# Loads in order of need, attention inside the first second-GEMM, and neighbouring chunks' GEMMs alternated, in a linear-attention plus two-GEMM kernel

## The chip, the cores and the metric

The kernel runs on one core of one Trainium2 chip. The metric is the time of one execution in device microseconds (us), as the median over several runs. In the profile the engines are PE (matrix multiply), PEld (its weight loads), DVE (vector engine), ACT (scalar engine), POOL (GpSimd) and SP (the engine that only issues transfers here). An engine's name with a trailing q (SPq, ACTq) is its transfer queue.

## The reference

Attention with exponential decay over 4 batches, 8 heads, 768 positions and head size 64 gives x, 3072 tokens by 512. Two GEMMs with an activation between them follow.

```python
# attention, per head, equivalent to:  out_i = sum_{j<=i} lam^(i-j) (q_i . k_j) v_j
x = attn_out.transpose(0, 2, 1, 3).reshape(3072, 512)
h = x @ w_in                                  # 512 x 2048
s = np.sin(alpha * h)
g = h + s * s / (alpha + 1e-09)
return (g @ w_out).astype(np.float32)         # 2048 x 512
```

## The kernel before

Tokens are worked in six chunks (c = 0 to 5) of 512. A chunk takes four attention steps of 128 tokens (s = 0 to 23), then 16 groups of GEMM1 (one for each 128 of the 2048 columns), then 16 groups of GEMM2 (4 for each 128 tokens). Every group is four matmuls of 128x512. The program only records operations with what they read and write and an assumed duration. A list scheduler then orders the queue of every engine by assumed readiness, except that PE keeps the program's order; semaphores are added at the end.

One attention step does this on the engines:

```python
def prep(s):                       # (cut to engine and operation)
    POOL: q2 = q32 * Lq            # scalings by powers of lam
    POOL: k2 = k32 * Lk
    ACT:  v2 = v32                 # cast to bf16
def att_T(s):  PE: 8 transposes of q2, k2;  DVE: qkT = copy from PSUM
def att_S(s):  PE: 8 score matmuls;         DVE: S_m = scores * mask
def att_O(s):  PE: output matmuls;          ACT: xT = copy from PSUM
               PE: state matmuls;           ACT: Zs = copy from PSUM (two of them)
```

The GEMM groups (cut):

```python
def grp_A(c, m):                   # GEMM1, one of 16 groups
    i = next_bank()                # ring of 5 PSUM banks
    PE:   m_ps[i] = 4 matmuls of w1, xT
    ACT:  t = sin(alpha * m_ps[i])
    POOL: u = t * t
    DVE:  gT[c % 2][m] = u * r + m_ps[i]
def grp_B(c, s4, m4, bank):        # GEMM2, one of 16 groups
    PE:   m_ps[bank] += 4 matmuls of gT, w2
    if m4 == 3:
        ACT: osb = copy of m_ps[bank]
        SP:  store osb
```

And the order (cut):

```python
load(0); consts(); load(1..3); alpha_ops()
for s in range(4):  prep, att_T, att_S, att_O of step s;  w1_block(s)
load(4); load(5)
for j in range(4): w2_block(j)     # two staging buffers, so block 2 waits for the cast of block 0
for s in range(6, 9): load(s)
for m in range(16): grp_A(0, m)
for m4 in range(4):
    for s4 in range(4): grp_B(0, s4, m4, banks[s4])
for s in range(4, 8): attention of step s          # nothing else for PE here
for c in range(1, 6):
    for m in range(16): grp_A(c, m)                # attention of chunk c+1 in between
    for s4 in range(4):
        bank = next_bank()
        for m4 in range(4): grp_B(c, s4, m4, bank) # alone on PE
```

## Time and profile before

The kernel took 272.02 us (median of three runs, 270.7 to 272.72). The profiled execution had a span of 270.4 us. I divide it by the first matmul of each stage in the timeline of PE.

| stage | from, us | length, us |
|---|---|---|
| before the first GEMM | 0 | 28.5 |
| GEMM1 of chunk 0 | 28.5 | 18.9 |
| GEMM2 of chunk 0, then attention of chunk 1 | 47.4 | 46.8 |
| GEMM1 of chunk 1 (attention of chunk 2 inside) | 94.2 | 23.4 |
| all the rest of PE's work | 117.6 | 149.7 |
| tail (last copy and store) | 267.3 | 3.1 |

These are lines of the profile's page of the kernel before. The first are busy time in us, share of the span and number of instructions of each engine. The digits are the busy share in tenths in 40 slices of the span, 6.8 us each. PEclk is the granted clock of PE in tenths, and GB/s is what the transfers moved. Of a group of instructions (engine, operation, destination, sources, shapes), the figures are the busy time in us and the mean ns of one, then the idle time ahead of them with what ended most of it.

```profile
span 270.4 us, 4030 instructions
PE 222.9 (82%) x1584; PEld 108.9 (40%) x1584; DVE 123.9 (46%) x159; ACT 120.7 (45%) x214; POOL 148.9 (55%) x151
...
PE   0346998822954699899999899999999999999895
...
POOL 1830299990043469990299930899206782069700
PEclk9995599995795579999999999999999999999999
DMA  8999999999999965655230012100121001210022
GB/s 164 220 209 393 240 292 269 205 238 335 209 219 283 229 153 119 156 119 155 78 80 0 2 39 78 41 1 2 40 78 41 0 2 39 78 41 0 0 78 78
...
L458 PE MATMUL m_ps<-w,gT 128*128 128x512 bf16 x384 | 87.1, 386 | 14.8 <-DVE w L343 12.8
```

Three things are to be seen. First (slices counted from 1), PE is partly idle in slices 1 to 4, and slices 9 to 14 hold a second hole. Second, the GEMM2 matmuls (L458) had 12.8 us of idle time that ended with a DVE weight cast. Third, the transfers are busy without a break for the first 95 us, and slices 2 and 3, which hold q, k and v loads, move 220 and 209 GB/s, where slice 4, with w1 blocks, moves 393. The q, k and v loads come in pieces of 256 bytes, the weights in pieces of 2 KB. The Trainium skill ("DMA: Bandwidth & Descriptors", Specifications) states that a transfer needs pieces of at least 512 bytes for the line rate, which these two rates agree with.

This is the chain of waits, which is followed back from the last instruction, for 56.9 to 66.3 us of the kernel before. Columns: start in us, length in us, what it was.

```profile
56.90 8.05 DMA w2s<-in_moe_w_out_dram
...
64.97 1.24 DVE w L343
...
66.25 9.17 PE m_ps L458 x32
```

GEMM2 of chunk 0 stops for its third weight block. After it, from 75.4 to 94.2, chunk 1's attention runs as a chain of short dependent steps with little for PE to do, and the granted clock was 0.54 from 80 to 90 us. The timeline of PE shows that idle time is in brackets:

```profile
76.66 0.40 PE L382 MATMUL A_ps<-qkT 64*128 64x128 bf16 x8 [0.79 <-DVE qkT L373]
78.38 0.40 PE L401 MATMUL A_ps<-qkT,Zs 128*128 128x128 bf16 x4 [1.32 <-DVE S_m L386]
```

In the long rest, GEMM1 is limited by POOL, which has 16 squares of 1.04 us in every chunk and, while the attention of a later chunk is prepared, up to 8 scalings of 1.04 us. The timeline of POOL in the kernel before shows them back to back:

```profile
102.93 1.04 POOL L350 TENSOR_TENSOR q_4<-q_2,Lq 128x512 bf16<-128x512 f32 x1
103.93 1.04 POOL L447 TENSOR_TENSOR u_0<-t_0 128x512 bf16<-128x512 bf16 x1
```

### The profile page before, as it was taken

The page shows a single profiled execution, that of the slowest core. Times are in us where ns is not written, and L with a number is a line of the kernel's source. Part 1 is how long each engine was busy: PE and PEld are TensorE (multiplying, and loading weights), DVE is VectorE, ACT ScalarE, POOL GpSimd, SP SyncE. Part 2 cuts the span into 40 slices and gives each one's busy share as a digit, 9 for nine tenths or more (in the row PEclk, how much of TensorE's full clock was granted, in tenths as well). Part 3 has the DMA queues.
Part 4 walks back from the last instruction along what each step waited for, and adds up shares of the span by engine and source line. Part 5 has one row for each costly group of instructions (what it writes and reads, how often), then busy time and mean ns, then how long its engine had stood idle before and what let it go on. Part 6 is the DMA issues. An engine that isn't in the chain of part 4 may idle for free.

```text
span 270.4 us, 4030 instructions
## 1 busy us (share of the span) xinstructions
PE 222.9 (82%) x1584; PEld 108.9 (40%) x1584; DVE 123.9 (46%) x159; ACT 120.7 (45%) x214; POOL 148.9 (55%) x151
## 2 busy tenths in 40 slices
PE   0346998822954699899999899999999999999895
PEld 0235432310433544444454444545445554443342
DVE  1246378601134358760187810787305893037600
ACT  2433477100132458731387711868216762167211
POOL 1830299990043469990299930899206782069700
PEclk9995599995795579999999999999999999999999
DMA  8999999999999965655230012100121001210022
GB/s 164 220 209 393 240 292 269 205 238 335 209 219 283 229 153 119 156 119 155 78 80 0 2 39 78 41 1 2 40 78 41 0 2 39 78 41 0 0 78 78
DMA packets 84786, 33.82 MB, mean 125 GB/s; under 512 B 77600, under 2 KB 77600, under 8 KB 84768
## 3 DMA queue, kind: packets, MB, share of 16 engines
q1 hardware_dynamic: 84768, 33.57, 51.5%
q8 instruction: 12, 0.20, 0.3%
q14 instruction: 6, 0.05, 0.1%
HBM read 27.28 MB, written 6.29 MB: 124 GB/s over the span
## 4 chain that ended last, share of the span: by engine, by line
PE 49%; POOL 18%; DVE 11%; DMA 7%; ACT 5%; SPq 5%; issue 4%; POOLq 1%; ACTq 0%
PE m_ps L458 25%; PE m_ps L441 15%; POOL u_2 L447 5%; SPq L290 4%; POOL u_1 L447 4%; DVE gT L449 4%; POOL u_0 L447 3%; POOL u_3 L447 3%; DVE S_m L386 3%; DMA w2s<-in_moe_w_out_dram 3%; PE A_ps L382 3%; DVE qkT L373 2%; DMA v_3<-in_v_dram 2%; DMA v_2<-in_v_dram 2%; PE A_ps L405 1%
## 5 line engine op out<-in xcount | busy, mean ns | idle before, releaser
L458 PE MATMUL m_ps<-w,gT 128*128 128x512 bf16 x384 | 87.1, 386 | 14.8 <-DVE w L343 12.8
L441 PE MATMUL m_ps<-xT,w 128*128 128x512 bf16 x384 | 94.4, 392 | 0.8 <-ACT xT L414 0.5
L447 POOL TENSOR_TENSOR u_0<-t_0 128x512 bf16<-128x512 bf16 x24 | 26.0, 1082 | 70.4 <-ACT t_0 L445 69.4
L458 PEld LDWEIGHTS m_ps<-w,gT 128*128 128x128 bf16 x384 | 37.1, 99 | 63.1 <-DVE w L343 14.2
L441 PEld LDWEIGHTS m_ps<-xT,w 128*128 128x128 bf16 x384 | 35.5, 100 | 46.5 <-DVE gT L449 6.9
L386 DVE TENSOR_TENSOR S_m<-A_ps,mask 128x1024 bf16<-128x1024 f32 x24 | 29.4, 1224 | 53.0 <-PE A_ps L382 52.9
L466 ACT COPY osb<-m_ps 128x512 f32<-128x512 f32 x24 | 14.1, 586 | 79.2 <-PE m_ps L458 77.4
L449 DVE SCALAR_TENSOR_TENSOR gT<-u_0,r_sb,m_ps 128x512 bf16<-128x512 bf16 x24 | 17.9, 744 | 24.3 <-POOL u_0 L447 24.2
L447 POOL TENSOR_TENSOR u_1<-t_1 128x512 bf16<-128x512 bf16 x24 | 26.0, 1082 | 1.3 <-ACT t_1 L445 1.3
L447 POOL TENSOR_TENSOR u_2<-t_2 128x512 bf16<-128x512 bf16 x24 | 25.0, 1041 | 1.1 <-ACT t_2 L445 0.6
L447 POOL TENSOR_TENSOR u_3<-t_3 128x512 bf16<-128x512 bf16 x24 | 25.0, 1041 | 0.0
L445 ACT ACTIVATE t_2<-m_ps,alpha_sb 128x512 bf16<-128x512 f32 x24 | 16.5, 687 | 15.0 <-PE m_ps L441 15.0
L449 DVE SCALAR_TENSOR_TENSOR gT<-u_2,r_sb,m_ps 128x512 bf16<-128x512 bf16 x24 | 17.9, 747 | 6.3 <-POOL u_2 L447 6.3
L449 DVE SCALAR_TENSOR_TENSOR gT<-u_1,r_sb,m_ps 128x512 bf16<-128x512 bf16 x24 | 17.9, 746 | 4.9 <-POOL u_1 L447 4.9
L373 DVE COPY qkT<-A_ps 128x1024 bf16<-128x1024 bf16 x20 | 13.7, 686 | 13.9 <-PE A_ps L370 13.9
L445 ACT ACTIVATE t_0<-m_ps,alpha_sb 128x512 bf16<-128x512 f32 x24 | 16.5, 687 | 6.0 <-PE m_ps L441 5.8
L449 DVE SCALAR_TENSOR_TENSOR gT<-u_3,r_sb,m_ps 128x512 bf16<-128x512 bf16 x24 | 17.8, 742 | 2.3 <-POOL u_3 L447 2.3
L445 ACT ACTIVATE t_1<-m_ps,alpha_sb 128x512 bf16<-128x512 f32 x24 | 16.5, 687 | 4.8 <-PE m_ps L441 4.7
L445 ACT ACTIVATE t_3<-m_ps,alpha_sb 128x512 bf16<-128x512 f32 x24 | 16.5, 687 | 4.8 <-PE m_ps L441 4.5
L382 PE MATMUL A_ps<-qkT 64*128 64x128 bf16 x192 | 11.0, 242 | 7.4 <-DVE qkT L373 6.6
L414 ACT CAST xT<-A_ps 128x512 bf16<-128x512 f32 x20 | 11.6, 579 | 11.4 <-PE A_ps L405 11.4
L428 ACT CAST Zs<-Z_ps 64x256 bf16<-64x256 f32 x40 | 14.7, 367 | 0.5
(164 smaller groups left out, 175.5 us busy)
## 6 DMA issues: line engine op xcount, KB each, us to landing
out_dram<-osb SPq DMA_DIRECT2D x24, 256.0 KB, 2.0
w1s<-in_moe_w_in_dram SPq DMA_DIRECT2D x4, 1024.0 KB, 8.5
w2s<-in_moe_w_out_dram SPq DMA_DIRECT2D x4, 1024.0 KB, 8.3
q_0<-in_q_dram SPq DMA_DIRECT2D x4, 256.0 KB, 4.6
k_0<-in_k_dram SPq DMA_DIRECT2D x4, 256.0 KB, 4.3
v_0<-in_v_dram SPq DMA_DIRECT2D x4, 256.0 KB, 5.4
q_1<-in_q_dram SPq DMA_DIRECT2D x4, 256.0 KB, 4.6
k_1<-in_k_dram SPq DMA_DIRECT2D x4, 256.0 KB, 4.9
```

The source lines that it names most:

```text
L290: rec("SP", lambda e, a=a, d=dst[r]: e.dma_start(d[:, :, :], a), 0, writes=[f"{nme}32.{r}"], slot=f"{nme}{r}", nbytes=128 * 2048)
L373: rec("DVE", lambda e: e.tensor_copy(qkT[j][:, :, :], dst), 0.7, reads=[key], writes=[f"qkT.{j}"])
L382: last = e.matmul(A_ps[:, 4 * h + jp, :], qkT[j][rows, 4 + jp, :], qkT[j][rows, jp, :])
L386: rec("DVE", lambda e: e.tensor_tensor(S_m[j][:, :, :], A_ps[:, :, :], mask_b, ALU.mult), 1.25, reads=["S0", "S1", "mask"], writes=[f"S_m. ...
L414: rec("ACT", lambda e: e.copy(xT[x][:, :, col:col + 128], dst), 0.62, reads=[key], writes=[f"x.{x}.{s % 4}"])
L428: rec("ACT", lambda e, rows=rows, cols=cols: e.copy(Zs[j][rows, :, cols], Z_ps[rows, :, :]), 0.4, reads=["Z"], writes=[f"Zs.{j}"])
L441: last = e.matmul(m_ps[i][:, :], w1[:, kc, 128 * m:128 * (m + 1)], xT[x][:, kc, :], start=(kc == 0), stop=(kc == NKC - 1))
L445: rec("ACT", lambda e: e.activation(t16[tt][:, :], m_ps[i][:, :], ACTF.Sin, scale=alpha_sb[:, m:m + 1]), 0.7, reads=[f"m.{i}", "alpha"], w ...
L447: rec("POOL", lambda e: e.tensor_tensor(u16[tt][:, :], t16[tt][:, :], t16[tt][:, :], ALU.mult), 1.05, reads=[f"t.{tt}"], writes=[f"u.{tt}"])
L449: rec("DVE", lambda e: e.scalar_tensor_tensor(out=gT[g][:, m, :], in0=u16[tt][:, :], scalar=r_sb[:, m:m + 1], in1=m_ps[i][:, :], op0=ALU.m ...
L458: last = e.matmul(m_ps[bank][:, :], gT[g][:, m, 128 * s4:128 * (s4 + 1)], w2[:, m, :], start=(m == 0), stop=(m == NM - 1))
L466: rec("ACT", lambda e: e.copy(osb[o][:, :], m_ps[bank][:, :]), 0.6, reads=[f"m.{bank}"], writes=[f"o.{o}"])
```

## The change

The intent is to give PE work where it waits. Loads are put in the order in which they are needed. Chunk 1's attention is placed between the groups of chunk 0's GEMM2. From then on GEMM1 of the next chunk alternates with GEMM2 of this one, so that POOL's work for GEMM1 is spread over twice the matmuls. Smaller parts: four q scalings and eight squares go from POOL to DVE, one staging ring of six serves both weights, alpha arrives as 16 rows and is transposed on PE, the stores are issued by ACT instead of SP, and the output buffers go from three to four.

The core of the diff (cut; the bookkeeping of the soft ordering between loads and the constants' changes are left out; comments after # are mine):

```diff
-            for nme, src, dst in (("q", q, q32), ("k", k, k32), ("v", v, v32)):
+            for nme, src, dst in (("k", k, k32), ("q", q, q32), ("v", v, v32)):
...
-        w1s = ring("w1s", 4, [128, NKC, 512], F32)
-        w2s = ring("w2s", 2, [128, 4, DM], F32)
+        ws = ring("ws", 6, [128, 4, 512], F32)
...
+            dve = c in (0, NCH - 1) and m % 4 == 3
+            rec("DVE" if dve else "POOL",
+                lambda e: e.tensor_tensor(u16[tt][:, :], t16[tt][:, :], t16[tt][:, :], ALU.mult),
+                0.35 if dve else 1.05, reads=[f"t.{tt}"], writes=[f"u.{tt}"])
...
-                rec("SP", lambda e: e.dma_start(out[row0:row0 + 128, :], osb[o][:, :]), 0,
+                rec("ACT", lambda e: e.dma_start(out[row0:row0 + 128, :], osb[o][:, :]), 0,
...
+        for s in range(4):
             load(s)
         alpha_ops()
+        for j in range(4):
+            w1_block(j)
+        for j in range(2):
+            load(4 + j)
+            w2_block(j)
+        loaded = [8]
...
+        def slot_att(base, i, per):      # attention step base + i // per, in parts
+            s = base + i // per
+            if s >= NSTEP:
+                return
+            if i % per == per // 4:
+                att_S(s)
+            elif i % per == per // 4 * 3:
+                att_O(s)
+                if s + 1 < NSTEP:
+                    att_T(s + 1)
+                prep_next(s + 2)         # also issues the next load
...
+            if s < 2:                    # within the steps of chunk 0
+                load(6 + s)
+                w2_block(2 + s)
...
         for m4 in range(4):
             for s4 in range(4):
                 grp_B(0, s4, m4, banks[s4])
+                slot_att(4, 4 * m4 + s4, 4)
+        for m in range(NM):
+            grp_A(1, m)
+            slot_att(8, m, 4)
         for c in range(1, NCH):
+            for i in range(NM):
+                if c + 1 < NCH:
+                    grp_A(c + 1, i)
+                    slot_att(4 * (c + 2), 2 * i, 8)
+                if i % 4 == 0:
+                    bank = next_bank()
+                grp_B(c, i // 4, i % 4, bank)
+                if c + 1 < NCH:
+                    slot_att(4 * (c + 2), 2 * i + 1, 8)
```

## The prediction

> **What bounds the kernel now.** Overview: PE 222.9 of 270.4 us (82%). The chain of waits shows three regimes.
> 1. Start, 0 to 28.5 us: no GEMM. Loads of steps 0-3 (256-byte pieces) move about 215 GB/s (overview, slices 2-3); weight loads reach 393. The Trainium skill ("DMA: Bandwidth & Descriptors", Specifications) asks for pieces of at least 512 B; the trace agrees. Landed inputs wait in order: Lk (7.6 us) behind v_0's cast and lam; qkT of step 2 behind alpha (18.2); xT behind v_3's cast.
> 2. 47 to 94 us: the third w2 block lands only at 65, behind later q/k/v loads: PE idles 10.2 us, returns at half clock (0.51 in 60-70), and chunk 1's attention runs as a bare latency chain from 75.5 to 94.
> 3. GEMM1 with attention and q/k scaling: POOL squares and scales at 1.04 us each, 16+8 are 25 us; three such phases took 26.4, 24.6 and 23.9 us, the fourth, free of scalings, 19.9 at PE's pace. GEMM2 takes 13.9 (217 ns a matmul), POOL mostly idle.
>
> **What changes.** Loads in order of need (alpha and lam off that queue; alpha as 16 rows instead of 2,048 four-byte pieces); four q scalings and 8 squares to DVE; stores issued by ACT; chunk 1's attention inside GEMM2 of chunk 0; GEMM1 of c+1 alternated with GEMM2 of c. Arithmetic is nearly unchanged. PE's warm floor: 768 x 217 ns + 24 x 1.5 us (attention step: (19.9-13.9)/4) = 203 us.
>
> **Estimate, from those durations.**
> - Same load rates: four steps land by 16-17 us, scaling constants come before v_0's cast: first GEMM at 23 (was 28.5).
> - GEMM1 of chunk 0: 12 squares and 3 scalings on POOL, weight casts and gT on DVE: ends near 41.
> - w2 interleaved with steps 4-7, the last lands near 53. GEMM2 with four attention steps, 19.9: ends near 62. Bare attention (18.5 us) and the 10 us wait disappear.
> - GEMM1 of chunk 1: POOL's order puts the scalings of steps 8-11 before its first square; step 11 lands near 68, so PE fills five banks and stalls 3.5 us; then 25 POOL operations: ends near 92 (was 120.8).
> - Three alternating chunks: POOL needs 25 us, PE 33.8: 101.
> - A new wait: the second GEMM gets the same bank each time, so its next group waits for the output copy, which ACT runs behind xT, two Zs and the v cast: estimate 0.5 us per attention step, 6.
> - GEMM1 of 5 with GEMM2 of 4: 28; last GEMM2 14; tail 3.
> Sum 244 us of span, less a little if the copy fits behind a GEMM1 group; time was 1.6 above span. I say 243.
>
> Nearly all is on the critical path, since PE becomes the limit: about 29 us before 121 us, the rest from POOL's slow chunks.
>
> **Predicted:** 243 us, 233 to 252 eight times in ten. Faster by over 2%: 0.97; within 2%: 0.02; slower: 0.01.
>
> **What would show it.** First GEMM at 21-25 us; no later PE gap over 4 us; chunk 1's attention between GEMM2 matmuls; PE above 90% busy from 95 us; alternating chunks at 34-36 us; GEMM2 waits for the ACT copy once per attention step; PE busy 205-215 us, clock 0.5 only before 35 us.
>
> **What would make it wrong.** Store issues on ACT holding up sines; DVE's added two-input work blocking POOL (its square took 2.0 us beside a weight cast, else 1.04), slowing GEMM1 of chunks 0 and 1; steps 8-11 landing after 68, as stores share the engines. Better: no bank wait and no stall before step 11 (about 235).

## The result, and the profile after

The changed kernel took 247.4 us (median of 4 runs, 245.79 to 248.81), beside 272.37 us for the kernel before. The ratio is 0.9092, with a 95% interval of 0.9023 to 0.916. A ratio is the mean time of one kernel's fast runs over the mean time of the other's in the same rounds, so it is not quite the ratio of the medians quoted. The profiled span was 245.2 us. All runs gave correct results. Executions over 1.5% slower than the fastest of the same kernel are left out of the means.

These are the lines of the page after that answer to those shown of before:

```profile
span 245.2 us, 3912 instructions
PE 218.0 (89%) x1560; PEld 107.9 (44%) x1585; DVE 132.2 (54%) x170; ACT 120.9 (49%) x215; POOL 141.9 (58%) x141
...
PE   0576969589989789999999999999999999999994
...
POOL 3220588973739799998668686554454445554100
PEclk9999988959999979999999999999999999999999
DMA  7999999999999799999311011011101100111122
GB/s 147 218 254 389 284 262 255 262 288 244 219 281 242 176 224 220 208 245 209 100 45 43 0 45 44 0 45 43 45 0 43 45 19 23 43 45 43 43 86 86
...
L478 PE MATMUL m_ps<-w,gT 128*128 128x512 bf16 x367 | 93.6, 385 | 1.8 <-ACT osb L486 0.5
```

The second hole of PE is gone: GEMM2's matmuls waited 1.8 us in all. (The attention's score matmuls that now stand between them, L400, waited 6.7 us in the whole kernel; the longest of these waits is taken up below.) From slice 16 on PE is full, and POOL's digits are 6 to 9 up to slice 25 and then 4 or 5 as long as GEMM1 runs, where they swung between 0 and 9 before. The transfers are nearly full until about 116 us (19 slices of 6.1 us), and POOL, the old limit, has spare time. The line of PE has 24 instructions fewer than the 1584 of before because matmul records are missing; the arithmetic is nearly the same.

The view of windows gives the busy time of each engine (and its number of instructions) in each stretch, then the granted clock, the DMA share and GB/s. Read PE, and PEclk. The kernel after, with the stages as its boundaries:

```profile
core 0: us, PE busy (x) PEld busy (x) DVE busy (x) ACT busy (x) POOL busy (x), PEclk, DMA share, GB/s
0.00:24.10 24.10, 11.58 (x141) 8.69 (x143) 12.54 (x19) 10.52 (x23) 5.49 (x13) 1.00 1.08 250
24.10:44.20 20.10, 17.91 (x63) 6.92 (x64) 16.09 (x19) 11.20 (x18) 15.54 (x13) 0.92 0.99 270
44.20:71.80 27.60, 23.16 (x202) 12.17 (x203) 15.96 (x18) 9.20 (x19) 18.22 (x16) 0.88 1.19 256
71.80:96.50 24.70, 21.48 (x196) 11.46 (x200) 16.67 (x22) 18.25 (x35) 21.06 (x22) 0.93 1.01 222
96.50:242.10 145.60, 143.83 (x960) 68.61 (x976) 70.95 (x95) 71.18 (x124) 81.55 (x80) 1.00 0.26 66
```

The same view of the kernel before, for the rest (cut 0.6 us later than in the table):

```profile
118.20:267.40 149.20, 144.86 (x974) 68.52 (x972) 69.36 (x91) 70.75 (x124) 81.21 (x81) 1.00 0.13 44
```

| stage | before, us | after, us | difference |
|---|---|---|---|
| before the first GEMM | 28.5 | 24.1 | -4.4 |
| GEMM1 of chunk 0 | 18.9 | 20.1 | +1.2 |
| GEMM2 of chunk 0 and attention of chunk 1 | 46.8 | 27.6 | -19.2 |
| GEMM1 of chunk 1 | 23.4 | 24.7 | +1.3 |
| the rest | 149.7 | 145.6 | -4.1 |
| tail | 3.1 | 3.1 | 0 |

So three quarters of the 25.2 us came out of one stage, and the alternation, which is the diff's last loop, touched a stage that gave 4.1. PE idled only 149.20 - 144.86 = 4.3 us in that stage before, although POOL limited GEMM1 there. GEMM2 followed each time with POOL nearly free, and most of the delay of one half was made good in the other.

### The profile page after: what moved, and what is told of

The parts are those of the page before. It is cut to its first block, busy times and chain, and to the rows that moved or that the text cites. A ratio compares the mean times of both kernels' runs of the same rounds, so it can differ in the third digit from the quotient of the medians.

```text
span 245.2 us, 3912 instructions
## 1 busy us (share of the span) xinstructions
PE 218.0 (89%) x1560; PEld 107.9 (44%) x1585; DVE 132.2 (54%) x170; ACT 120.9 (49%) x215; POOL 141.9 (58%) x141
## 4 chain that ended last, share of the span: by engine, by line
PE 72%; ACT 5%; DMA 5%; DVE 5%; POOL 5%; SPq 4%; issue 3%; ACTq 0%; POOLq 0%
PE m_ps L478 33%; PE m_ps L459 27%; SPq L305 4%; PE A_ps L400 3%; DMA v_0<-in_v_dram 3%; PE A_ps L423 2%; DMA q_3<-in_q_dram 2%; PE A_ps L386 2%; DVE gT L469 2%; DVE w L361 1%; POOL u_1 L467 1%; PE A_ps L419 1%; POOL u_2 L467 1%; PE A_ps L388 1%; POOL u_0 L467 1%
## 5 line engine op out<-in xcount | busy, mean ns | idle before, releaser
L459 PE MATMUL m_ps<-xT,w 128*128 128x512 bf16 x376 | 99.1, 396 | 4.6 <-DVE gT L469 2.0
L478 PE MATMUL m_ps<-w,gT 128*128 128x512 bf16 x367 | 93.6, 385 | 1.8 <-ACT osb L486 0.5
L459 PEld LDWEIGHTS m_ps<-xT,w 128*128 128x128 bf16 x384 | 38.0, 101 | 51.8 <-issue 6.8
L478 PEld LDWEIGHTS m_ps<-w,gT 128*128 128x128 bf16 x384 | 34.6, 99 | 43.7 <-ACT osb L486 6.6
L467 POOL TENSOR_TENSOR u_0<-t_0 128x512 bf16<-128x512 bf16 x24 | 26.1, 1089 | 33.0 <-ACT t_0 L463 33.0
L467 POOL TENSOR_TENSOR u_2<-t_2 128x512 bf16<-128x512 bf16 x24 | 25.8, 1077 | 16.0 <-ACT t_2 L463 15.9
L467 POOL TENSOR_TENSOR u_1<-t_1 128x512 bf16<-128x512 bf16 x24 | 25.4, 1058 | 8.3 <-ACT t_1 L463 8.3
L469 DVE SCALAR_TENSOR_TENSOR gT<-u_2,r_sb,m_ps 128x512 bf16<-128x512 bf16 x24 | 17.9, 747 | 20.1 <-POOL u_2 L467 20.1
L463 ACT ACTIVATE t_2<-m_ps,alpha_sb 128x512 bf16<-128x512 f32 x24 | 16.5, 687 | 24.7 <-PE m_ps L459 24.6
L467 POOL TENSOR_TENSOR u_3<-t_3 128x512 bf16<-128x512 bf16 x16 | 16.6, 1040 | 7.9 <-ACT t_3 L463 7.8
L400 PE MATMUL A_ps<-qkT 64*128 64x128 bf16 x192 | 10.6, 236 | 6.7 <-DVE qkT L391 6.7
```

What stands on the lines that cost most here:

```text
L400: last = e.matmul(A_ps[:, 4 * h + jp, :], qkT[j][rows, 4 + jp, :], qkT[j][rows, jp, :])
L459: last = e.matmul(m_ps[i][:, :], w1[:, kc, 128 * m:128 * (m + 1)], xT[x][:, kc, :], start=(kc == 0), stop=(kc == NKC - 1))
L463: rec("ACT", lambda e: e.activation(t16[tt][:, :], m_ps[i][:, :], ACTF.Sin, scale=alpha_sb[:, m:m + 1]), 0.7, reads=[f"m.{i}", "alpha"], w ...
L467: lambda e: e.tensor_tensor(u16[tt][:, :], t16[tt][:, :], t16[tt][:, :], ALU.mult),
L469: rec("DVE", lambda e: e.scalar_tensor_tensor(out=gT[g][:, m, :], in0=u16[tt][:, :], scalar=r_sb[:, m:m + 1], in1=m_ps[i][:, :], op0=ALU.m ...
L478: last = e.matmul(m_ps[bank][:, :], gT[g][:, m, 128 * s4:128 * (s4 + 1)], w2[:, m, :], start=(m == 0), stop=(m == NM - 1))
```

## The experiments

My theory after the result was this. The 19.2 us came from two separate things: the third w2 block in time, and the attention no longer alone on PE. The alternation is worth only a few us. What is left behind is a queue of DVE work ahead of one attention copy in GEMM2 of chunk 0, and late v loads in front of ACT's sines in GEMM1 of chunk 1. The rivals: the load order alone made the gain, or the alternation did; and what is left behind comes from the shared PSUM banks, the squares moved to DVE, or ACT's time to issue stores. Each text below was on record before its run, and its letters belong to that text's question.

All edits are made on the changed kernel. "Before" in the table is the kernel before in the same rounds. Every ratio is against that.

| run | edit | median, us | before, us | ratio (95% interval) |
|---|---|---|---|---|
| changed kernel | | 247.4 | 272.37 | 0.9092 (0.9023 to 0.916) |
| e1_loads_only | no attention in GEMM2, no alternation | 259.61 | 271.08 | 0.9575 (0.9513 to 0.9638) |
| e2_no_alternation | no alternation | 249.89 | 271.08 | 0.922 (0.9174 to 0.9266) |
| e3_attention_after | no attention in GEMM2 | 254.51 | 271.08 | 0.9358 (0.929 to 0.9426) |
| e4_late_w2 | last two w2 blocks behind later loads | 252.02 | 271.08 | 0.9298 (0.9259 to 0.9338) |
| e5_squares_pool | all squares on POOL | 247.38 | 271.45 | 0.9105 (0.9056 to 0.9154) |
| e6_stores_sp | stores issued by SP | 242.52 | 271.45 | 0.8933 (0.891 to 0.8956) |
| e7_own_banks | own PSUM banks for GEMM2 | 248.24 | 271.45 | 0.9146 (0.9123 to 0.917) |
| e8_w2_cast_act | w2 casts on ACT | 244.55 | 271.45 | 0.8937 (0.8873 to 0.9) |
| e9_v_late | v casts later in ACT's queue | 248.3 | 272.13 | 0.9124 (0.9076 to 0.9172) |
| e10_act_vlate | e8 and e9 | 246.1 | 272.13 | 0.9049 (0.9005 to 0.9094) |
| e11_sp_vlate | e6 and e9 | 244.36 | 272.13 | 0.8981 (0.8946 to 0.9016) |
| e12_all | e6, e7 mended, e8 and e9 | 239.41 | 272.13 | 0.8805 (0.8767 to 0.8842) |

### The three parts of the change apart

e1 undoes both moves of PE's order, e2 only the alternation, e3 only the attention in GEMM2. Together with the changed kernel they are a two by two.

```diff
 # e1 and e3
                 grp_B(0, s4, m4, banks[s4])
-                slot_att(4, 4 * m4 + s4, 4)
+        for i in range(16):
+            slot_att(4, i, 4)
 # e1 and e2: for each c the groups of GEMM2 first, then
+            if c + 1 < NCH:
+                for m in range(NM):
+                    grp_A(c + 1, m)
+                    slot_att(4 * (c + 2), m, 4)
```

> The changed kernel with both re-orderings of PE work undone: chunk 1's attention runs after the first second-GEMM, and GEMM2 of c is followed by GEMM1 of c+1. Loads, constants, stores and moved squares stay changed. Theory A (the attention filling is the main gain): about 258 us, so the load part is worth some 14 us and the two re-orderings some 11. Rival B (the loads are nearly everything, since the old kernel waited 10 us for w2 and ran attention cold): 250 or less. The stretch from the first GEMM2 matmul to the first GEMM1 matmul of chunk 1 should be 36 to 38 us under A (before 46.8, after 27.6).

> The changed kernel with only the alternation undone. Theory A (POOL's excess in a GEMM1 phase was already mostly paid back in the GEMM2 phase that followed; from the start of the second chunk's GEMM2 to the end the kernel before took 149.8 us and the changed one 145.6): 250 to 252 us, so 3 to 5 us slower than the change. Rival B, as the recorded prediction reads it (POOL's slow phases cost their full 5 us per chunk and the last one 4.6): 256 or more.

> The changed kernel with chunk 1's attention again after the first GEMM2, the alternation kept. With e1 and e2 this makes a square of four. If the two parts are independent, it is e1 plus the change minus e2: about 254 if e1 is 258 and e2 251. If the attention filling is the main re-ordering, it is at least 6 us slower than the change.

Measured, as differences of ratios with 1% being 2.71 us: the loads and the small parts give 4.25% (11.5 us). The attention in GEMM2 gives a further 3.6% (9.6 us) without alternation and 2.7% (7.2 us) with it. The alternation gives 2.2% (5.9 us) without the attention in GEMM2 and 1.3% (3.5 us) on top of it. The three steps 4.25 + 3.55 + 1.28 make up the 9.1% of the whole. So no single part made the gain. By the intervals each of these differences is sure to about 2 or 2.5 us only, so that 9.6 and 7.2, or 5.9 and 3.5, are not clearly different. e1, e2 and e3 came out near what their texts had first (about 258, 250 to 252 and about 254).

The traces agree on where. The stage "GEMM2 of chunk 0 and attention of chunk 1" was 46.8 us in before, 38.8 in e1, 25.6 in e2 and 27.6 after; it ended at 94.2, 82.0, 72.0 and 71.8 us. The rest was 148.7 us in e1 and 148.1 in e2, both without alternation, and 145.6 in e3 and after, with it.

The two things that I had called separate overlap here. Where GEMM2 of chunk 0 runs without the attention it needs the w2 blocks earlier, and PE waited for their casts again: 4.9 us in e1 and 3.2 in e3, not at all in the changed kernel. So a part of what the attention in GEMM2 is worth is time for the loads, and not only the end of the bare chain.

### The w2 blocks

e4 brings the last two w2 blocks back behind the loads of steps 6 to 9.

```diff
-            if s < 2:
-                load(6 + s)
-                w2_block(2 + s)
+            if s == 3:
+                for n in range(6, 10):
+                    load(n)
+                w2_block(2)
+                w2_block(3)
```

> The changed kernel with the third and fourth w2 blocks loaded after steps 6 to 9, as the kernel before had them, instead of between. Theory A (order of need matters only where nothing else waits: the third block now lands 9 us before it is used, because GEMM2 starts late and is filled with attention): 1 to 3 us slower than the change. Rival B (the w2 order is what removed the 10 us wait): at least 6 us slower, with PE idle over 5 us inside the first GEMM2.

Measured: 252.02 us, 2.1% (5.6 us) over the changed kernel by the ratios. This lay between what the two theories gave. The timeline of PE in e4 has the old wait back, in a smaller size:

```profile
64.39 2.22 PE L478 MATMUL m_ps<-w,gT 128*128 128x512 bf16 x6 [4.21 <-DVE w L361]
```

So early w2 blocks account for about half of the 11.5 us that the loads and small parts give, if they are worth as much there as here, with the other parts of the change in place. The first GEMM starts 4.4 us earlier, which would be most of the other half; I did not take that apart further.

### What is left in GEMM2 of chunk 0

This stage took 27.6 us where I had allowed 21. PE idled 4.4 us of it (27.60 - 23.16), and ran at half clock for some time after. The timelines of PE, then of DVE, of the changed kernel show why. First PE:

```profile
50.23 0.61 PE L400 MATMUL A_ps<-qkT 64*128 64x128 bf16 x8 [3.70 <-DVE qkT L391]
50.77 3.60 PE L478 MATMUL m_ps<-w,gT 128*128 128x512 bf16 x8
```

And DVE:

```profile
46.85 0.73 DVE L469 SCALAR_TENSOR_TENSOR gT<-u_2,r_sb,m_ps 128x512 bf16<-128x512 bf16 x1
47.51 1.40 DVE L361 CAST w<-ws 128x2048 bf16<-128x2048 f32 x1
48.83 0.74 DVE L469 SCALAR_TENSOR_TENSOR gT<-u_3,r_sb,m_ps 128x512 bf16<-128x512 bf16 x1
49.49 0.68 DVE L391 COPY qkT<-A_ps 128x1024 bf16<-128x1024 bf16 x1
```

PE had finished its transposes for step 4 at 44.8 and had only eight matmuls of GEMM2 in hand after them. The copy of the transposes' result stood last in DVE's queue, behind GEMM1's last groups and a weight cast, and PE, which works in order, stood behind the copy. Then eight matmuls took 3.60 us; eight take 1.89 us in the steady stream. The Trainium skill ("TensorE: Matmul & The Clock Gate", Part 1) states that PE falls to half clock after an idle window of about 3.4 us; the near doubling here agrees with it. The 3.4 us are no threshold for a gap, though. In windows of 1 us the granted clock of the changed kernel falls at 35.3, 49.0 and 86.5 us, and the gaps of PE there were 1.99, 3.70 and 2.25 us; in e12 a gap of 2.95 us (to 35.71) was not followed by a fall.

Two experiments touch DVE's queue. e8 moves the four w2 casts to ACT, e5 moves the eight squares back to POOL.

```diff
 # e8
-            rec("DVE", lambda e: e.tensor_copy(w2[:, 4 * j:4 * (j + 1), :], ws[i][:, :, :]), 1.2,
+            rec("ACT", lambda e: e.copy(w2[:, 4 * j:4 * (j + 1), :], ws[i][:, :, :]), 2.0,
 # e5
-            dve = c in (0, NCH - 1) and m % 4 == 3
+            dve = False
```

> The changed kernel with the four w2 casts on ACT instead of DVE. Theory A (in GEMM1 of chunk 0 and at the start of GEMM2 the limit is DVE's queue: weight casts of 1.2 to 2.0 us in front of gT and qkT, and a POOL square beside a cast takes 2.0 us): GEMM2 of chunk 0 starts about 2 to 3 us earlier, its 3.7 us wait for qkT falls under 1.5, total 3 to 5 us faster. Rival B (the loads are the limit until about 90 us: what is won there is lost again where ACT waits for v of steps 12 to 14): the start of GEMM1 of chunk 1 moves, but the total is less than 1.5 us faster, and GEMM1 of chunk 1 gets longer.

> The changed kernel with all squares on POOL again (8 of them were on DVE, 4 in chunk 0 and 4 in the last). Theory A (DVE is the fuller engine in GEMM1 of chunk 0: 16.1 busy of 20.1 us, and its squares make POOL wait): within 1.5 us of the change, either way. Rival B (POOL is the limit of chunk 0, four squares more cost their 4.2 us): 3 to 4 us slower, and the stretch of GEMM1 of chunk 0 grows from 20 to 23 us. The last chunk's part should be nothing, as it now shares PE with GEMM2.

e8 measured 244.55 us. That is 4.2 us less than the changed kernel by the ratio of its two fast runs, and 2.0 us less by the medians of all four, each beside the kernel before of its rounds. Two of its four runs are slow, one of them the profiled one, because its fastest run was 241.28; their clocks of 0.979 and 0.985 are like the others', so I read this as scatter and do not rest more than a sign on it. In its trace the 3.70 us wait is gone and the stage took 22.4 us at full clock. The two other kernels with this edit, profiled in fast runs, had 23.9 (e10) and 24.3 us (e12) for it, both at full clock, and e11 without it has the 3.70 us wait again. So the theory of the DVE queue holds for the wait. Its other half does not: GEMM2 of chunk 0 was to start 2 to 3 us earlier, and started at 44.5 us in e8, 42.8 in e10 and 43.7 in e12, beside 44.6 in the changed kernel and 43.75 in e11 (first matmuls of GEMM2). And GEMM1 of chunk 1 then took 28.1 us instead of 24.7. More than half of what was gained was given back there, which is taken up below.

e5 measured 247.38 us, ratio 0.9105 beside 0.9092: the eight squares moved to DVE made no difference that shows. The wait changed its place: GEMM1 of chunk 0 grew from 20.1 to 24.3 us, the 4.2 us that rival B had, at its end with a wait of 5.15 us for POOL's scaling of q. But GEMM2, whose first matmul came 4.5 us later, at 49.1, then took 23.2 us without the 3.70 us wait, and ended at 72.4 us beside 71.8.

### What is left in GEMM1 of chunk 1

In the changed kernel ACT stood behind v casts whose loads had not landed, with the sines of GEMM1 queued after them. The timeline of ACT after:

```profile
77.51 0.62 ACT L372 CAST v_2<-v_0 128x512 bf16<-128x512 f32 x1 [0.18 <-DMA v_0<-in_v_dram]
...
82.38 0.62 ACT L372 CAST v_3<-v_1 128x512 bf16<-128x512 f32 x1 [2.57 <-DMA v_1<-in_v_dram]
```

PE paid for it with an idle stretch and a spell of low clock (timeline of PE after):

```profile
86.23 0.40 PE L400 MATMUL A_ps<-qkT 64*128 64x128 bf16 x8 [2.25 <-DVE qkT L391]
86.97 3.14 PE L459 MATMUL m_ps<-xT,w 128*128 128x512 bf16 x7 [0.34 <-issue]
```

Two cures were tried. e6 puts the stores back on SP. e9 keeps everything but records each v cast from step 12 on one step later, behind the latest sine.

```diff
 # e6
-                rec("ACT", lambda e: e.dma_start(out[row0:row0 + 128, :], osb[o][:, :]), 0,
+                rec("SP", lambda e: e.dma_start(out[row0:row0 + 128, :], osb[o][:, :]), 0,
 # e9 (cut): the cast split out of prep(s)
-                prep_next(s + 2)
+                prep_next(s + 2, with_v=s + 2 < 12)
+                if 12 <= s + 1 < NSTEP:
+                    prep_v(s + 1)          # ACT cast, soft-ordered after the last sine
```

> The changed kernel with the output stores issued by the sync engine again. An issue on ACT took 0.34 to 0.5 us in the trace, 24 of them are 9 us of ACT time, but ACT is 49% busy. Theory A (they cost PE nothing, and on the load queue a store that waits for its copy holds the loads behind it): the same within 1 us to 3 us slower. Rival B (store issues on ACT delay the output copies and sines, and with them PE): 2 us or more faster.

e6 measured 242.52 us, 1.6% (4.3 us) less than the changed kernel by the ratios. That is the number of rival B, but not by its cause. The stage windows of e6, for GEMM1 of chunk 1 and the rest, answer to the last two of the changed kernel's:

```profile
70.70:91.70 21.00, 20.06 (x197) 11.10 (x202) 16.46 (x21) 18.34 (x34) 19.80 (x21) 1.00 1.16 244
91.70:237.20 145.50, 143.83 (x960) 68.57 (x976) 71.53 (x95) 71.04 (x123) 82.94 (x82) 1.00 0.30 71
```

GEMM1 of chunk 1 fell from 24.7 to 21.0 us, and no v cast in this stage waits any more. The rest is the same (145.5 and 145.6), although 20 of the 24 stores lie in it. GEMM2 of chunk 0, at whose end ACT issued the first four, took 27.2 us from its first matmul in the changed kernel and 26.9 in e6. So the time that ACT needs to issue stores costs nothing that shows. What differs is when chunk 0's four stores, 1 MB, enter the transfer engines. The transfer queue's timeline of the changed kernel has the first at

```profile
67.70 0.37 ACTq L489 DMA_DIRECT2D out_dram<-osb  x1
```

and in e6 the first three lines of SP from that store on are

```profile
81.27 0.92 SPq L489 DMA_DIRECT2D out_dram<-osb  x1
82.23 0.43 SPq L305 DMA_DIRECT2D v<-in_v_dram  x1
82.70 1.85 SPq L489 DMA_DIRECT2D out_dram<-osb  x3
```

In SP's queue the stores stood behind loads that were already in line, and the v load of step 13 was issued at 73.15 us instead of 76.39. In ACT's own queue they went ahead of those loads, while the loads were still the limit (the page shows the DMA share at 7 to 9 tenths until about 116 us). From 66 to 78 us the transfers moved 3.2 MB in the changed kernel, of which 1.05 MB were the four stores, and 2.6 MB in e6, all of them loads. The Trainium skill ("DMA: Bandwidth & Descriptors", Issuing engines are not separate DMA queues) states that transfers issued from different engines run on the same 16 transfer engines and interleave, and that only time on the issuing sequencer is saved. e6 agrees with the sharing: the second queue saved nothing here and cost 4 to 5 us.

> The changed kernel with the v casts of step 12 and later placed one step later in ACT's order, behind sines that are issued first; stores stay on ACT. In the changed kernel ACT waited 0.2, 2.6 and 0.9 us for v of steps 12 to 14, with sines of chunk 1 behind those casts. Theory A (these waits in ACT's order stretch GEMM1 of chunk 1, and the stores on SP helped in e6 only because they fell behind those loads): 3 to 5 us faster than the change, GEMM1 of chunk 1 at most 22.5 us (24.7 in the change, 21.8 in e6). Rival B (e6 was faster because store issues take ACT's time, or because stores take PE-side time elsewhere): under 1.5 us faster.

e9 measured 248.3 us, ratio 0.9124: no gain, and my theory, that a cast behind the sines would free the stage, fell as a cure. Its profiled execution fell into a slow run of 322.14 us, so there is no trace of a fast one, and e9 by itself stays unexplained. The two combinations tell part of it. (The texts of e9 and e10 count GEMM1 of chunk 1 to the first GEMM2 matmul after it, 0.9 us later than I do here, when they say 21.8 us for e6 and 29.0 for e8; their 24.7 for the changed kernel is counted as here.)

```diff
 # e10 = e8's edit and e9's;   e11 = e6's edit and e9's
```

> w2 casts on ACT (e8) and late v casts (e9). In e8 GEMM1 of chunk 1 started 4.9 us earlier but took 29.0 instead of 24.7 us. Theory A (it met the loads of steps 12 to 14 earlier, so ACT waited longer for v): with the late casts that phase takes 22 to 24 us and the total is 238 to 241, 6 us or more faster than the change. Rival B (the casts on ACT slow that phase by themselves, or POOL and the q and k scalings wait for the same loads): 242 or more.

> Both, stores on SP (e6) and late v casts (e9). Theory A (one cause, two cures): as fast as e6 within 1.5 us, about 242. Rival B (two causes): the gains add, 239 or less.

e10 measured 246.1 us (e8 alone 244.55), e11 244.36 us (e6 alone 242.52). In neither did the late casts help, and both missed their theory A. In e10's trace GEMM1 of chunk 1 starts early, at 66.75, and the wait is now POOL's. Its timeline:

```profile
69.59 1.04 POOL L372 TENSOR_TENSOR q<-q,Lq 128x512 bf16<-128x512 f32 x1 [1.76 <-DMA q<-in_q_dram]
72.62 1.04 POOL L370 TENSOR_TENSOR k<-k,Lk 128x512 bf16<-128x512 f32 x1 [1.99 <-DMA k<-in_k_dram]
73.62 3.04 POOL L474 TENSOR_TENSOR u<-t 128x512 bf16<-128x512 bf16 x3
```

No square could be taken before 73.62, PE idled 2.58 and 1.01 us, and the stage took 27.9 us. This is the stall before step 11 that the prediction named. It appears only when the stage before it ends early enough; in the changed kernel that ended at 71.8 and the loads had landed. So the stage is limited by the loads whichever engine stands in front, and what e8 gains ahead of it is partly lost in it. The ends of the stage say the same. With the stores on ACT it started at 66.75 (e10), 66.9 (e8), 71.8 (changed kernel) and 72.4 (e5), and ended at 94.6, 95.0, 96.5 and 96.8 us; with the stores on SP it started at 68.0 (e12), 70.5 (e11) and 70.7 (e6), and ended at 91.4, 92.9 and 91.7.

### The PSUM banks of the alternating part

The prediction allowed 6 us for GEMM2 groups that wait until ACT has copied their bank. In the changed kernel such waits are on the weight load queue, not on PE. The view of waits (engine and line, what ended them, us in total, times, longest) for 100 to 240 us shows, for the weight loads and then for PE:

```profile
PEld m_ps L478 <- ACT osb L486: 6.6, 15, 0.8
```

```profile
PE m_ps L478 <- ACT osb L486: 0.5, 2, 0.3
```

The weight load of the next group waited 6.6 us, while PE was busy with matmuls that had been issued already, and PE itself waited 0.5 us. e7 gives GEMM2 two banks of its own and GEMM1 the other three.

```diff
-                    grp_A(c + 1, i)
+                    grp_A(c + 1, i, (16 * (c - 1) + i) % 3)
...
-                    bank = next_bank()
+                    bank = 3 + (4 * c + i // 4) % 2
```

> The changed kernel where GEMM2 of the alternating part owns two accumulator banks in turn and GEMM1 the other three. Theory A (GEMM2's next group waits about 0.2 to 0.3 us per attention step for the output copy of the group before, as it gets the same bank): 1.5 to 3 us faster; waits of GEMM2's weight loads on the output copy (6.6 us now) fall under 1 us. Rival B (three banks are too few for the chain of sine, square and gT, near 3 us): as fast or slower, with new waits of GEMM1 on gT.

e7 measured 248.24 us, ratio 0.9146. It was no faster. The waits of the weight loads for the copies are gone from its trace, but my edit made a new one: the first group of the alternating part got the bank of the last group of the phase before it and waited 2.64 us for gT, at the end of GEMM1 of chunk 1. Then PE's clock fell to half, inside the rest. The timeline of PE, and the window of the rest, in e7:

```profile
99.81 1.91 PE L478 MATMUL m_ps<-w,gT 128*128 128x512 bf16 x4
101.52 1.76 PE L459 MATMUL m_ps<-xT,w 128*128 128x512 bf16 x4
...
98.80:244.00 145.20, 144.21 (x960) 70.15 (x976) 68.56 (x91) 70.72 (x122) 79.47 (x78) 0.99 0.25 62
```

From 99.81 to the next instruction at 103.21 these eight matmuls took 3.4 us, and eight at full clock take 1.7 us from start to start. So of the 145.2 us some 1.7 are the half clock, and without it the rest would have taken about 143.5 us (an estimate), 2 us less than the 145.6 of the changed kernel. So the bank wait was worth about 2 us, more than the 0.5 us that PE's own waits show. e12 below tests it again.

### All that helped, together

e12 takes the stores on SP, the w2 casts on ACT, the late v casts and own banks. The new wait of e7 is mended by shifting GEMM1's bank by one.

```diff
-                    grp_A(c + 1, i)
+                    grp_A(c + 1, i, (16 * (c - 1) + i + 1) % 3)
```

> w2 casts on ACT, late v casts, stores on SP, and GEMM2 of the alternating part in two banks of its own, now with the bank that was freed first given to the first GEMM1 group (in e7 that group got the bank of the last group of the phase before and PE waited 2.6 us there). Theory (the bank wait is hidden by matmuls in flight: PE idled only 1.5 us in 120 us of the alternating part): within 1.5 us of e10, 237 to 240 us. If the bank wait had been real on PE, as the recorded prediction has it (6 us), it would be 234 or less.

e12 measured 239.41 us, ratio 0.8805 (0.8767 to 0.8842). It beats both kernels: 12% below the kernel before, and 3.2% (8 us) below the changed one by the medians. The stage windows from GEMM2 of chunk 0 on:

```profile
43.70:68.00 24.30, 21.11 (x196) 10.51 (x196) 11.90 (x14) 14.78 (x23) 10.55 (x12) 1.00 0.91 225
68.00:91.40 23.40, 22.24 (x201) 11.44 (x201) 16.26 (x21) 16.84 (x31) 22.60 (x23) 0.93 1.17 245
91.40:235.30 143.90, 143.68 (x976) 69.64 (x976) 71.10 (x95) 72.61 (x126) 83.39 (x82) 1.00 0.30 76
```

GEMM2 of chunk 0 runs at full clock, and in the rest PE idles 0.2 us of 143.9. Against e11, which lacks the ACT casts and the own banks, the first of these stages is 2.5 us shorter, the second 1 us longer and the rest 2.6 us shorter. It was the own banks that shortened the rest. e10 has the ACT casts and the late v casts but no own banks, and its rest took 146.4 us:

```profile
94.60:241.00 146.40, 145.35 (x976) 68.55 (x976) 70.49 (x94) 72.78 (x126) 83.05 (x82) 1.00 0.25 68
```

In the six profiled kernels with alternation but neither own banks nor late v casts (the changed one, e3, e4, e5, e6 and e8) the rest took 145.5 or 145.6 us. So the ACT casts do nothing there (e8), the late v casts cost about 1 us (e10 and e11: 146.4 and 146.5), and the own banks gain 2.5 us on top (143.9). The theory of e12 thus had its number right, 237 to 240 us, and its reason wrong: e12 is 6.7 us below e10 and not within 1.5, 4.5 us of it in GEMM1 of chunk 1, where the stores on SP count, and 2.5 in the rest.

## Why the prediction was right or wrong

The prediction said 243 us, in a range from 233 to 252, and faster with 0.97. Measured were 247.4 us. It was right in the size, but the sum came out close partly because misses of 3 to 7 us cancelled. Some of that has one cause (the loads, see GEMM1 of chunk 1); that the oversized bank term made up for the first two stages was luck. Against the profiled spans:

| term of the sum | predicted, us | measured, us | miss |
|---|---|---|---|
| first GEMM at | 23 | 24.1 | +1.1 |
| GEMM1 of chunk 0 (ends 41) | 18 | 20.1 | +2.1 |
| GEMM2 of chunk 0 with attention (ends 62) | 21 | 27.6 | +6.6 |
| GEMM1 of chunk 1 (ends 92) | 30 | 24.7 | -5.3 |
| three alternating chunks, bank wait, the last two parts (101 + 6 + 28 + 14) | 149 | 145.6 | -3.4 |
| tail | 3 | 3.1 | +0.1 |
| sum | 244 | 245.2 | +1.2 |

- **The start** was right to 1 us. The loads moved at the rates that I had taken from before, 218 and 254 GB/s in slices 2 and 3, and the scaling constants came in time.
- **GEMM1 of chunk 0** was 2.1 us longer, and the warning under "what would make the prediction wrong" had named half of a cause that the trace shows. POOL squares at 31.41 and 40.51 us took 2.06 and 1.96 us beside DVE weight casts, the others of this stage 1.03 to 1.31. (The warning blamed the added two-input work of DVE; the long squares stand beside casts, as they did before, where one took 2.02 us.) The Trainium skill ("SBUF — State Buffer", Who interferes with whom) states that DVE copies and casts in a two-port mode, when they start first, lock POOL out of the port pair that they share for the whole instruction; these two durations agree with it. PE's one long wait in the stage was 1.99 us, for a gT that stood in DVE's queue behind a w1 cast (1.22 us), a square moved to DVE (1.26 us there, 0.58 for the stage's other squares on DVE) and another gT; then the clock was half for 3.4 us. What each of these cost isn't taken apart. The moved squares as such did not lengthen the stage: without them (e5) it took 24.3 us.
- **GEMM2 of chunk 0** is the largest miss. I took 19.9 us from a free-running phase of before, and this one isn't free-running: a copy queued behind DVE's other work held PE for 3.70 us. Of the 27.6 us, 21.1 is PE's work at full clock (as in e12), about 2.1 the slower clock (23.16 - 21.11), and 4.4 idle time. e8 supports it: with the casts off DVE the stage fell to 22.4 (23.9 and 24.3 in e10 and e12). My sign "no later PE gap over 4 us" was nearly broken.
- **The bare attention and the w2 wait** disappeared as predicted, and that is where most of the gain is. e1, e2 and e3 show that placing attention in GEMM2 was worth 7 to 10 us, 3 to 5 of it waits for w2 that it hides, and e4 that early w2 blocks were worth 5.6.
- **GEMM1 of chunk 1** was 5.3 us shorter than predicted. The stall that I had put before step 11 did not come, because the stage started 9.8 us later than I had it (71.8 instead of 62). This is not luck of a separate kind: the loads set when this stage can end, so a delay before it was hidden. When e10 moved the start to 66.75, the stall came, with 2.58 and 1.01 us of idle PE, where 3.5 was predicted. In the changed kernel the loads show instead in ACT's v casts, and e6 shows that 3.7 us of the stage came from the stores' place among the loads. The prediction had "stores share the engines" among its risks, but no term for it.
- **The bank wait** of 6 us was the wrong size in the alternating part. The mechanism is there, and once per attention step as predicted (12 of the 15 waits, the others in the part without attention). But the 6.6 us of waiting are on the weight load queue, while PE had matmuls in hand, and without them the part was only 2 us shorter (e7, with the half clock taken out) to 2.5 us (e12 against e10).
- **The alternation** was worth 3.5 to 6 us (e1, e2, e3), less than a reader expects who counts 25 us of POOL in each GEMM1. POOL's excess in GEMM1 had been mostly made good in the GEMM2 that followed, and it was smaller than the prediction read (last point).
- **The signs**: the first GEMM at 21 to 25 us, PE above 90% busy from 95 us (143.83 of 145.60 us after 96.5), no gap over 4 us and alternating chunks at 34 to 36 us (35.3, 34.7 and 33.9 from first sine to first sine) came true. PE's busy time of 218.0 us was over the 205 to 215 named, and the clock was half after 35 us too (35.3 to 38.7, 49.0 to 55.8 and 86.5 to 89.9 us), which I had ruled out.
- **A reading error**: I gave 120.8 us as the end of GEMM1 of chunk 1 in before. The timeline has the first GEMM2 matmul after it at 117.6; 120.8 is the second piece of that GEMM2. So the gain ahead of this point was 117.6 - 96.5 = 21.1 us, not about 29. The same slip is in "26.4, 24.6 and 23.9 us": each counts the first 12 matmuls of the GEMM2 that follows, and from first matmul to first matmul the three phases took 23.4, 21.9 and 21.3 us, beside 19.9 for the one without scalings. So POOL's excess was 1.3 to 3.5 us a chunk, and not 4 to 6.5. The predicted total doesn't depend on it.

What stays open: why e9's late v casts gave nothing by themselves, since no trace of a fast run exists (in e10 and e11 they cost about 1 us in the rest); what each small part at the start is worth; and what made GEMM1 of chunk 0 longer.

## What to carry to other kernels

Before you count a slow half as a loss, look whether the following half makes it good: PE's idle time over both is what an interleaving can win, 4.3 us here, and not the 5 us a chunk that a count of POOL suggests (25 us beside 19.9 of PE). When a stage is placed inside another, cost it with the queues that it will meet there: one copy behind a weight cast held an in-order PE for 3.7 us, and the half clock came with it. While loads were the limit here, stores on a second queue went ahead of loads that the program would rather have had first; in the loads' queue they cost 4.3 us less. And look for what your own edit adds before you call an effect small: the bank wait seemed worth 0.4 us (145.6 and 145.2) until the half clock that e7 had made was taken out.

## What the Trainium skill lacked or had wrong

- "TensorE: Matmul & The Clock Gate", Part 1, states that the activity gate grants half or full clock only, and adds 13/16 for a die with three loaded cores and a note of a gate stuck at a quarter. One execution of e9, on one core, fits none of these. It took 322.14 us at a mean granted clock of 0.681. Its page shows 6 tenths in every slice from the fifth on, and windows of 1 us show a steady 0.65, with PE busy 94% of the time and GEMM matmuls of 516 and 508 ns on average, where the changed kernel has 396 and 385. What set this clock the record does not tell. The line of that execution's page:

```profile
PEclk9997666666666666666666666666666666666666
```

- "DMA: Bandwidth & Descriptors", Specifications, states a least size for the line rate. Its section on small descriptors gives an overhead for 256 bytes (27%), but I found no measured read rate on trn2 for such pieces on the queue that SP issues; the runs show 209 to 220 GB/s in the slices that hold q, k and v loads alone, against up to 393 GB/s with 2 KB pieces, 44 to 47% less.
- The same page, "Issuing engines are not separate DMA queues", says that a second issuing engine saves little. Neither it nor the page's account of how the engines take turns between queues says that it can cost: its transfers go ahead of loads that wait in the first engine's queue. Here four stores of 256 KB each cost 4.3 us by the ratios (e6).
- Part 1 of the TensorE page gives the fall to half clock after an idle window of about 3.4 us. Here gaps of 1.99 and 2.25 us were enough in the changed kernel, while one of 2.95 us in e12 brought no fall. It has no figure for how much work in a window still counts as idle.
- What "SBUF — State Buffer" states of the port lock and Part 1 of the halved clock agreed with the traces (2.06 us for a square otherwise 1.03 to 1.31; 3.60 us for eight matmuls otherwise 1.89).
